# A spectral layer and a feed-forward network in one kernel: stage 1 of the first batch handed on within SBUF, and the start-up ranked anew

## The chip, the cores and the metric

The kernel runs on one core of a Trainium2 chip. The metric is the device time of one execution in microseconds: the median of three runs for the kernel before the change. In what follows PE is TensorE's matmul, PEld its weight load, DVE is VectorE, ACT is ScalarE, POOL is GpSimd, SP is SyncE, which here issues most DMAs. "L305" is line 305 of the kernel before the change.

## The reference

```
x: (8, 3008, 256) float32;  w_r, w_i: (256, 256);  b_r, b_i: (256)
X = rfft(x, axis=1)                               # along the sequence of 3008
Yr = Xr @ w_r - Xi @ w_i + b_r
Yi = Xr @ w_i + Xi @ w_r + b_i
Y  = soft threshold of both with lam = 0.01
y  = irfft(Y, n=3008, axis=1)                     # (8, 3008, 256), taken as 24064 tokens

h = y @ w_in                                      # w_in (256, 2048)
g = h * clip(h + 3, 0, 6) / 6
out = g @ w_out                                   # w_out (2048, 256), out (24064, 256) float32
```

The inputs `w_in` and `w_out` arrive as float64 and are decoded on the chip.

## The kernel before, in words

The sequence of 3008 is split into 64 x 47, so that the transform is one of length 47 and one of length 64. Half the spectrum is kept, NK = 24 of the 47 frequencies. The 64 rows are taken in seven sets (`SEGS`): six of 10 rows and one of 4. A set of 10 rows fills 120 partitions (5 rows x 24) with two groups of 256 columns.

For each batch b three stages make y:

- `stage1(b)` (L264): a set of x is loaded (`xin`, the part for "plus" and the part for "minus" side by side, 4 KB in a row), sum and difference are made, and a matmul with the tables of length 47 gives the cosine part (c = 0) and the sine part (c = 1). ACT copies each into a tile `a` (L303), and a DMA stores it to the DRAM scratch `scr1` (L305). For batch 0 this is plain fp32 without `split`, the stores are issued from ACT's queue, and `a` uses seven tags of other buffers in turn.
- `middle(b)` (L353): 12 steps over pairs of frequencies. Each loads `bt` from `scr1` (L367), where the 128 partitions are now (c, n1), and a table `f64` (L368); `s2` makes the transform of length 64 (L376); `s3` the mixing with w_r and w_i (L137, from `mixed`), bias and soft threshold (L414, L425, L426, L429), and turns the halves over into `zt` by four small DMAs within SBUF (L439), for the last two pairs of batch 0 by four DVE copies (L437); `s5` goes back over the length 64 (L453), is copied by ACT into `pt` (L455) and stored to `scr2` (L456).
- `segment(b, k)` (L477): loads `qt` from `scr2` (L486), goes back over the length 47 (L505) and writes y into `raw` (L513, L515, L527).

`prepare(c)` (L544) then makes the combinations of 512 tokens that the network wants, in tiles `yb`. The network runs over 376 units (47 blocks of 512 tokens x 8 slices f of the 2048 hidden columns): `phase_a` to `phase_d` multiply by `w_in` with seven products of half size in place of eight, `gate` makes the activation, and `down` multiplies by `w_out` (L631). Every fp32 operand is split into a high and a low part (`split`, L128: an ACT cast and a subtraction), and a product is three matmuls.

The weights are decoded in 16 bands of 512 KB: `in_band(f)` and `out_band(f)` for f = 0 to 7, in the order in0, in1, out0, in2, out1, in3, out2, in4, ... Each is a load `st` from SP (L178) and work on DVE, ACT and POOL (L190 to L222). `turn()` (L244) brings bands on; `EARLY` and `LATE` say in which borrowed buffers. Unit f needs in_band(f), and three units later out_band(f).

The order of the work in each engine's queue is not simply the order of the text. The framework schedules the instructions over a simulated timeline with the text's order as priority: an instruction whose operands and buffers are free earlier can be drawn ahead. `tc.high_priority()` ranks what it encloses first. After that the queues are fixed: each engine and each DMA-issuing queue works in order.

The start is written out by hand: stage 1 of batch 0, then the 36 steps of `middle(0)` with a `turn` every third, then the first two segments with `turn(LATE)` between, then `prepare(0)` (L647 to L663), then the loop over the units, in which `fill` places the later batches' stages at computed slots.

Of the kernel before, what the change touches and what calls it, by code (L numbers as in the profile page):

```python
# [1 line left out]

# [1 line left out]

# [5 lines left out]
F32 = mybir.dt.float32  # L10
F32R = mybir.dt.float32r
# [10 lines left out]
B, S, D, FF = 8, 3008, 256, 2048  # L22
N1, N2 = 64, 47
NK = N2 // 2 + 1
LAM = 0.01
P = 128

J = 5
SEGS = tuple((n1, min(2 * J, N1 - n1)) for n1 in range(0, N1, 2 * J))
R47 = J * NK  # L30
# [70 lines left out]
def spectral_ffn(ctx: ExitStack, tc: tile.TileContext, x, w_r, w_i, bias, w_in, w_out, f47, f64, g64, sgn, out):  # L101
    nc = tc.nc
    const = ctx.enter_context(tc.tile_pool(name="const", bufs=1))
    sb = ctx.enter_context(tc.tile_pool(name="sb", bufs=1))
    dram = ctx.enter_context(tc.tile_pool(name="dram", bufs=2, space=DRAM))
# [8 lines left out]
    def space(shape, dt, name, tag=None):  # L114
        tag = tag or name
        return sb.tile(shape, dt, name=name, tag=tag, bufs=depth.get(tag, 1))
# [11 lines left out]
    def split(hi, lo, src, on=None):  # L128

        nc.scalar.copy(out=hi, in_=src)  # L130
        (on or nc.vector).tensor_tensor(out=lo, in0=src, in1=hi.bitcast(F32), op=ALU.subtract)  # L131

    def product(ps, terms, start=True, stop=True, more=False):

        todo = [p for (ah, al), (bh, bl) in terms for p in ((al, bh), (ah, bl), (ah, bh))]
        for n, (a, b) in enumerate(todo):
            nc.tensor.matmul(  # L137
                out=ps,
                lhsT=a,
                rhs=b,  # L140
                start=start and n == 0,
                stop=stop and n == len(todo) - 1,
                skip_group_check=more,
            )
# [9 lines left out]
    def run(g):  # L154
        for _ in g:
            pass

    nf = NFT // 2
# [5 lines left out]

    win_s = [const.tile([P, nf, 7, P], F32R, name="w_in_" + t) for t in ("hi", "lo")]
    wout_s = [const.tile([P, NFT * D], F32R, name="w_out_" + t) for t in ("hi", "lo")]

    top = const.tile([P, 2], F32, name="top")  # L170
# [32 lines left out]
    def in_band(f, tags):  # L203
        def cut(t, words):
            v = t.rearrange("p (h c) -> p h c", h=2)
            return v[:, :, f * 256 * words : (f + 1) * 256 * words]

        w, s = yield from decode(w_in, cut, tags)
        s = s.rearrange("p a (b c) -> p (a b) c", b=2)
        a11, a12, a21, a22 = w[:, 0, :P], w[:, 1, :P], w[:, 0, P:], w[:, 1, P:]  # L210
        for to, a, b, op in (
            (0, a21, a22, ALU.add),
            (1, s[:, 0], a11, ALU.subtract),
            (2, a11, a21, ALU.subtract),
            (3, a12, s[:, 1], ALU.subtract),
        ):
            nc.gpsimd.tensor_tensor(out=s[:, to], in0=a, in1=b, op=op)
        yield
        hi, lo = (t[:, f] for t in win_s)
        split(hi[:, :2], lo[:, :2], w[:, :, :P])  # L220
        split(hi[:, 2], lo[:, 2], a22)
        split(hi[:, 3:], lo[:, 3:], s)  # L222
# [10 lines left out]
    EARLY = (("raw", "yb", "yb", "yb"),)  # L233
# [10 lines left out]
    def turn(how=None):  # L244

        for job in list(busy):
            if next(job[0], busy) is busy:
                busy.remove(job)
                ready.add(job[1])
        if how and made[0] < 2 * nf:  # L250
            make, f = next(bands)
            g = make(f, how[made[0] % len(how)])
            next(g)
            busy.append((g, (make, f)))
            made[0] += 1
# [6 lines left out]
    scr1, scr2 = {}, {}  # L262

    def stage1(b):  # L264
        scr1[b] = dram.tile([2, N1, NK, D], F32, name="scr1")
        sets = SEGS[-1:] + SEGS[:-1]
        xins = {}

        def load(i):
            n1, n = sets[i]  # L270
            rows, w = (R47, 2 * D) if n == 2 * J else (n * NK, D)
            tag = ("xin", "gs", None, "gs", None, "raw", "raw")[i] if b == 0 else "xin"
            if tag == "gs":
                xins[i], xins[i + 1] = twin([P, 2, 2 * D], F32, "xin", tag)
            elif tag:
                xins[i] = space([P, 2, 2 * D], F32, "xin", tag)
            at = n1 // J * 2 * D
            src = x[b, :rows, at : at + 2 * w].rearrange("p (s c) -> p s c", s=2)
            nc.sync.dma_start(out=xins[i][:rows, :, :w], in_=src)
            return rows, w  # L280

        shapes = [load(i) for i in range(len(sets))] if b == 0 else [load(0)]
        for i, (n1, n) in enumerate(sets):
            rows, w = shapes[i]
            xin = xins.pop(i)
            plus, minus = xin[:rows, 0, :w], xin[:rows, 1, :w]
            e = space([P, 2 * D], F32, "e", "r" if b == 0 else "e")[:rows, :w]
            (nc.vector if b == 0 else nc.gpsimd).tensor_tensor(out=e, in0=plus, in1=minus, op=ALU.add)  # L288
            (nc.vector if b == 0 else nc.gpsimd).tensor_tensor(out=plus, in0=plus, in1=minus, op=ALU.subtract)
            for c, src in enumerate((e, plus)):  # L290
                q = 2 * i + c
                if b == 0:
                    ps = room(c == 1)
                    turns = f47_s[2][:rows, c * R47 : c * R47 + rows]
                    nc.tensor.matmul(out=ps[:rows, :w], lhsT=turns, rhs=src, start=True, stop=True)
                else:
                    xs = [t[:rows, :w] for t in twin([P, 2 * D], F32R, "xs")]
                    split(*xs, src, nc.vector if b == 1 else nc.gpsimd)
                    yield
                    ps = room()  # L300
                    product(ps[:rows, :w], [([t[:rows, c * R47 : c * R47 + rows] for t in f47_s[:2]], xs)])
                a = space([P, 2 * D], F32, "a", ("a", "h", "z", "h", "xs", "h", "X")[q % 7] if b == 0 else "a")[:rows, :w]
                nc.scalar.copy(out=a, in_=ps[:rows, :w])  # L303
                dst = scr1[b][c, n1 : n1 + n].rearrange("(g j) k d -> (j k) g d", g=w // D)
                (nc.sync if b else nc.scalar).dma_start(out=dst, in_=a.rearrange("p (g d) -> p g d", d=D))  # L305
                if c and b and i + 1 < len(sets):
                    shapes.append(load(i + 1))
                yield
# [26 lines left out]
    for i, _ in enumerate(stage1(0)):  # L335
        if i == 7:
            r, k = [loaded(w, P, 2 * D, n, "yb") for w, n in ((w_r, "w_r"), (w_i, "w_i"))]
# [14 lines left out]

    def middle(b):  # L353
        scr2[b] = dram.tile([2, N1, NK, D], F32, name="scr2")
        src = scr1[b].rearrange("c n k d -> (c n) k d")
        dst = scr2[b].rearrange("c n k d -> (c n) k d")
        NG = NK // 2
        LAG = (1, 2, 3) if b else (2, 5, 5)
        bt, xs, zs = {}, {}, {}
# [3 lines left out]
            return tags[0 if b else g % 3]  # L363

        def load(g):
            bt[g] = space([P, 2, D], F32, "bt"), space([P, 2, P], F32, "f64")
            nc.sync.dma_start(out=bt[g][0], in_=src[:, 2 * g : 2 * g + 2, :])  # L367
            nc.sync.dma_start(out=bt[g][1], in_=f64.rearrange("p (k c) -> p k c", c=P)[:, 2 * g : 2 * g + 2])  # L368

        def s2(g):  # L370
# [86 lines left out]

        load(0)
        load(1)
        for g in range(NG + LAG[2]):  # L460
            if g >= LAG[2]:
# [79 lines left out]
    WEIGHT = {1: 0, 2: 1, 3: 6, 4: 2, 5: 3, 6: 4, 7: 5}  # L541
    yb = {}

    def prepare(c):  # L544
        y = raw.pop(c)
        b11, b12, b21, b22 = y[:, 0, :H], y[:, 0, H:], y[:, 1, :H], y[:, 1, H:]
        s = space([P, 4, H], F32, "T")
        for to, p, q in ((0, b12, b11), (1, b22, s[:, 0]), (2, b22, b12), (3, b21, s[:, 1])):
            nc.gpsimd.tensor_tensor(out=s[:, to], in0=p, in1=q, op=ALU.subtract)
        yield  # L550
        for n, src in ((2, b21), (1, b11), (6, s[:, 1]), (7, s[:, 2]), (5, s[:, 0]), (4, s[:, 3]), (3, b22)):
            t = space([P, 2, H], F32R, "yb")
            split(t[:, 0], t[:, 1], src, nc.vector if c == 0 and n in (1, 2) else nc.gpsimd)
            yb[c, n] = (t[:, 0], t[:, 1])
            yield
# [3 lines left out]

    def block(i, n, ps, start):  # L560
        c, f = units[i]
        product(ps, [(tuple(t[:, f, WEIGHT[n]] for t in win_s), yb[c, n])], start=start, more=True)

    def kept(i, n, ps):
        t = keep[i, n] = space([P, H], F32, n)
# [79 lines left out]


    mid = middle(0)  # L647
    for i in range(3 * (NK // 2)):
        next(mid)
        if i % 3 == 0:  # L650
            turn(EARLY if i == 3 or i % 9 == 0 else None)
    run(mid)
    first = [segment(0, k, tag) for k, tag in ((0, "qt"), (1, "h"))]
    for g in first:
        next(g)
    for n in range(3):
        turn(LATE)
        turn()
    for g in first:
        turn(LATE)  # L660
        run(g)
        turn()
    run(prepare(0))  # L663


    slots = {}
# [21 lines left out]
    for c in range(1, NC):  # L688
        g = prepare(c)
# [23 lines left out]
    n = len(units)  # L713
# [75 lines left out]
```

## Time and profile before

| | |
|---|---|
| median of three runs | 2643.61 us (2640.65 to 2645.09) |
| the profiled execution | 2643.59 us |
| its span | 2641.8 us |
| mean granted clock of TensorE | 0.988 |
| PE busy | 2562.4 us, 97% |
| PEld busy | 2291.9 us, 87% |
| DVE, ACT, POOL busy | 1975.7, 1820.1, 796.0 us |
| HBM read, written | 97.45 MB, 74.97 MB |

The span is the time from the first to the last instruction, 1.8 us less than the time of the same execution. The engines work side by side, so their busy times do not add up to the span. Lines of the timeline give the start, the time from the first start to the last end of a run of equal instructions, the engine, the line, the operation, written tile <- read tiles, shapes, the count, and in brackets the idle time of the engine before and what ended it. Lines of the waits give who waited for whom, the total, the number of times and the longest.

### The profile page before, as it was taken

The page shows a single profiled execution, that of the slowest core. Times are in us where ns is not written, and L with a number is a line of the kernel's source. Part 1 is how long each engine was busy: PE and PEld are TensorE (multiplying, and loading weights), DVE is VectorE, ACT ScalarE, POOL GpSimd, SP SyncE. Part 2 cuts the span into 40 slices and gives each one's busy share as a digit, 9 for nine tenths or more (in the row PEclk, how much of TensorE's full clock was granted, in tenths as well). Part 3 has the DMA queues.
Part 4 walks back from the last instruction along what each step waited for, and adds up shares of the span by engine and source line. Part 5 has one row for each costly group of instructions (what it writes and reads, how often), then busy time and mean ns, then how long its engine had stood idle before and what let it go on. Part 6 is the DMA issues. An engine that isn't in the chain of part 4 may idle for free.

```text
span 2641.8 us, 44527 instructions
## 1 busy us (share of the span) xinstructions
PE 2562.4 (97%) x16406; PEld 2291.9 (87%) x16406; DVE 1975.7 (75%) x3186; ACT 1820.1 (69%) x3592; POOL 796.0 (30%) x749
## 2 busy tenths in 40 slices
PE   5789999999999999999999999999999999999999
PEld 3577998988898998988898998999889889898887
DVE  7786886877677777777777777777777777666766
ACT  5476677767667777766776777677777666676766
POOL 2263334443233332233323333233321121121210
PEclk8889999999999999999999999999999999999999
DMA  7623333332223321323213322233221111100000
GB/s 216 191 79 93 103 104 94 113 107 75 59 60 96 88 69 48 85 78 90 73 49 86 88 76 63 76 84 84 63 79 58 50 53 53 43 26 30 12 17 17
DMA packets 150178, 199.98 MB, mean 76 GB/s; under 512 B 16847, under 2 KB 104135, under 8 KB 149959
## 3 DMA queue, kind: packets, MB, share of 16 engines
q1 hardware_dynamic: 146675, 193.98, 25.4%
q10 hardware_dynamic: 3284, 3.15, 0.4%
q8 instruction: 129, 2.11, 0.3%
q14 instruction: 90, 0.74, 0.1%
HBM read 97.45 MB, written 74.97 MB: 65 GB/s over the span
## 4 chain that ended last, share of the span: by engine, by line
PE 84%; DVE 4%; ACT 4%; DMA 2%; POOL 2%; issue 2%; SPq 0%; ACTq 0%; POOLq 0%; DVEq 0%
PE po L631 36%; PE pb L137 17%; PE ps_a L137 11%; PE pc L137 9%; PE pd L137 4%; PE ps_a L505 3%; PE ps_a L376 3%; ACT gs L130 1%; DMA xin<-in_x 1%; DVE r L610 1%; ACT r L608 1%; DVE gs L131 1%; POOL e L288 1%; DVE h L572 1%; POOL yb L131 0%
## 5 line engine op out<-in xcount | busy, mean ns | idle before, releaser
L631 PE MATMUL po<-gs,w_out_hi 128*128 128x512 f32 x3008 | 1006.5, 396 | 0.0
L610 DVE SCALAR_TENSOR_TENSOR r<-r,h 128x1024 f32<-128x1024 f32 x376 | 486.9, 1295 | 267.7 <-ACT r L608 265.9
L631 PEld LDWEIGHTS po<-gs,w_out_hi 128*128 128x128 f32 x3008 | 541.3, 188 | 85.5
L631 PE MATMUL po<-gs,w_out_lo 128*128 128x512 f32 x1504 | 601.9, 400 | 5.9 <-ACT gs L130 3.3
L608 ACT ACTIVATE r<-h,three 128x1024 f32<-128x1024 f32 x376 | 434.3, 1155 | 214.6 <-DVE h L572 211.6
L137 PE MATMUL pb<-yb,w_in_hi 128*128 128x256 f32 x3008 | 571.6, 279 | 2.5 <-POOL yb L131 2.5
L131 DVE TENSOR_TENSOR gs<-r,gs 128x1024 fp32r<-128x1024 f32 x376 | 484.4, 1288 | 80.7 <-ACT gs L130 78.8
L137 PEld LDWEIGHTS pb<-yb,w_in_hi 128*128 128x128 f32 x3008 | 461.0, 189 | 22.5 <-POOL yb L131 2.7
L130 ACT CAST gs<-r 128x1024 fp32r<-128x1024 f32 x376 | 395.8, 1053 | 92.5 <-DVE r L610 89.5
L572 DVE TENSOR_TENSOR h<-pc,u 128x256 f32<-128x256 f32 x752 | 315.1, 419 | 175.3 <-PE pc L137 160.1
L131 POOL TENSOR_TENSOR yb<-T,yb 128x256 fp32r<-128x256 f32 x188 | 181.0, 969 | 859.4 <-ACT yb L130 841.6
L137 PE MATMUL pb<-yb,w_in_lo 128*128 128x256 f32 x1504 | 431.3, 288 | 4.6 <-ACT p L567 1.6
L567 ACT COPY u<-pb 128x256 f32<-128x256 f32 x752 | 277.8, 373 | 121.5 <-PE pb L137 103.8
L631 PEld LDWEIGHTS po<-gs,w_out_lo 128*128 128x128 f32 x1504 | 284.0, 189 | 63.3 <-ACT gs L130 14.5
L137 PEld LDWEIGHTS pb<-yb,w_in_lo 128*128 128x128 f32 x1504 | 284.3, 189 | 29.7 <-ACT h L601 4.1
L137 PE MATMUL pc<-yb,w_in_hi 128*128 128x256 f32 x1504 | 297.6, 279 | 0.8 <-POOL yb L131 0.8
L137 PEld LDWEIGHTS pc<-yb,w_in_hi 128*128 128x128 f32 x1504 | 230.7, 189 | 13.3 <-POOL yb L131 1.1
L137 PE MATMUL pc<-yb,w_in_lo 128*128 128x256 f32 x752 | 219.0, 291 | 5.5 <-DVE h L572 4.9
L567 ACT COPY p<-pb 128x256 f32<-128x256 f32 x376 | 139.9, 372 | 80.9 <-PE pb L137 78.6
L601 ACT COPY h<-pb 128x256 f32<-128x256 f32 x376 | 140.5, 374 | 57.4 <-PE pb L137 55.4
L572 DVE TENSOR_TENSOR h<-pd,p 128x256 f32<-128x256 f32 x376 | 156.7, 417 | 14.9 <-ACT p L567 10.2
L137 PEld LDWEIGHTS pc<-yb,w_in_lo 128*128 128x128 f32 x752 | 142.1, 189 | 21.7 <-DVE h L572 7.9
(125 smaller groups left out, 3928.9 us busy)
## 6 DMA issues: line engine op xcount, KB each, us to landing
bt<-scr SPq DMA_DIRECT2D x96, 256.0 KB, 2.9
scr<-pt SPq DMA_DIRECT2D x96, 256.0 KB, 2.4
zt<-tc SPq DMA_DIRECT2D x376, 64.0 KB, 2.0
out<-ot SPq DMA_DIRECT2D x94, 256.0 KB, 2.3
xin<-in_x SPq DMA_DIRECT2D x48, 480.0 KB, 4.8
qt<-scr SPq DMA_DIRECT2D x96, 240.0 KB, 3.5
scr<-a SPq DMA_DIRECT2D x84, 240.0 KB, 2.5
f<-in_f SPq DMA_DIRECT2D x96, 128.0 KB, 2.8
```

Of the source, the lines that this page charges most:

```text
L130: nc.scalar.copy(out=hi, in_=src)
L131: (on or nc.vector).tensor_tensor(out=lo, in0=src, in1=hi.bitcast(F32), op=ALU.subtract)
L137: nc.tensor.matmul(out=ps, lhsT=a, rhs=b, start=start and n == 0, stop=stop and n == len(todo) - 1, skip_group_check=more,)
L288: (nc.vector if b == 0 else nc.gpsimd).tensor_tensor(out=e, in0=plus, in1=minus, op=ALU.add)
L376: nc.tensor.matmul(out=psv[:, dh, :, u, :], lhsT=data[:, u, dh * P : (dh + 1) * P], rhs=f[:, u, :], start=True, stop=True,)
L505: nc.tensor.matmul(out=ps[:, cs * w + g * rows : cs * w + (g + 1) * rows], lhsT=qt[:rows, cs, g, dh * P : (dh + 1) * P], rhs=f47_s[2][:row ...
L567: nc.scalar.copy(out=t, in_=ps)
L572: nc.vector.tensor_tensor(out=to, in0=ps, in1=keep.pop((i, n)), op=ALU.add)
L601: nc.scalar.copy(out=hs[i][:, 1, :H], in_=pb)
L608: nc.scalar.activation(out=r, in_=h, func=AF.Relu, bias=three, scale=1.0)
L610: nc.vector.scalar_tensor_tensor(out=r, in0=r, scalar=6.0, in1=h, op0=ALU.min, op1=ALU.mult)
L631: nc.tensor.matmul(out=pos[dh], lhsT=w[:, ft * D + dh * P : ft * D + (dh + 1) * P], rhs=g[:, low, u], start=f == 0 and u == 0 and which == ...
```

## The change

- Batch 0's stage 1 no longer goes through DRAM. Each result `a` is written by DMAs into an SBUF area `spread`, with (c, n1) on the partitions and 24 x 256 numbers in each: one DMA for each group of 5 rows, so that 120 partitions of 1 KB go into 5 partitions of 24 KB. Group 0 is issued from ACT, group 1 from SP. The copies out of PSUM and these DMAs are ranked first. `middle(0)` reads its pairs from `spread`, with no `bt` load.
- `spread` lies in the place of the `w_in` slices that are decoded last: high and low parts now share one tile, the low ones in reversed order, and `spread` covers positions 4 to 10 of 16: the high parts of f = 4 to 7 and the low parts of f = 7, 6 and 5. These can be written only when the last stage 2 product has read its pair.
- x is laid out with all "plus" parts of a row ahead of all "minus" parts, so a set is loaded as two packets of 2 KB for each partition instead of one of 4 KB.
- `EARLY` is used at seven of the 36 steps instead of five.
- The rest of `middle(0)` after the 36 steps, the first two segments and `prepare(0)` are ranked first.

```diff
-    win_s = [const.tile([P, nf, 7, P], F32R, name="w_in_" + t) for t in ("hi", "lo")]
+    win_t = const.tile([P, 2 * nf, 7, P], F32R, name="w_in")
+    win_s = [[win_t[:, f] for f in range(nf)], [win_t[:, 2 * nf - 1 - f] for f in range(nf)]]
+    spread = win_t[:, nf // 2 : nf // 2 + 7].rearrange("p f s c -> p (f s c)").bitcast(F32)
+    spread = spread[:, : NK * D].rearrange("p (k d) -> p k d", d=D)
...
-            at = n1 // J * 2 * D
-            src = x[b, :rows, at : at + 2 * w].rearrange("p (s c) -> p s c", s=2)
+            at = n1 // J * D
+            src = x[b, :rows].rearrange("p (s c) -> p s c", s=2)[:, :, at : at + w]
...
-                nc.scalar.copy(out=a, in_=ps[:rows, :w])
-                dst = scr1[b][c, n1 : n1 + n].rearrange("(g j) k d -> (j k) g d", g=w // D)
-                (nc.sync if b else nc.scalar).dma_start(out=dst, in_=a.rearrange("p (g d) -> p g d", d=D))
+                with tc.high_priority() if b == 0 else nullcontext():
+                    nc.scalar.copy(out=a, in_=ps[:rows, :w])
+                if b:
+                    dst = scr1[b][c, n1 : n1 + n].rearrange("(g j) k d -> (j k) g d", g=w // D)
+                    nc.sync.dma_start(out=dst, in_=a.rearrange("p (g d) -> p g d", d=D))
+                else:
+                    for g in range(w // D):
+                        at = c * N1 + n1 + g * J
+                        queue = nc.sync if g else nc.scalar
+                        with tc.high_priority():
+                            queue.dma_start(out=spread[at : at + rows // NK], in_=a[:, g * D : (g + 1) * D])
...
-            bt[g] = space([P, 2, D], F32, "bt"), space([P, 2, P], F32, "f64")
-            nc.sync.dma_start(out=bt[g][0], in_=src[:, 2 * g : 2 * g + 2, :])
+            bt[g] = space([P, 2, D], F32, "bt") if b else spread[:, 2 * g : 2 * g + 2], space([P, 2, P], F32, "f64")
+            if b:
+                nc.sync.dma_start(out=bt[g][0], in_=src[:, 2 * g : 2 * g + 2, :])
...
-            turn(EARLY if i == 3 or i % 9 == 0 else None)
-    run(mid)
+            turn(EARLY if i == 0 or i % 6 == 3 else None)
+    def ahead(g):
+        with tc.high_priority():
+            run(g)
+
+    ahead(mid)
     first = [segment(0, k, tag) for k, tag in ((0, "qt"), (1, "h"))]
     for g in first:
-        next(g)
+        with tc.high_priority():
+            next(g)
...
-        run(g)
+        ahead(g)
         turn()
-    run(prepare(0))
+    ahead(prepare(0))
...
-    pairs = half[:, :, :12].reshape(B, R47, 6, 2, 2, D).transpose(0, 1, 2, 4, 3, 5)
-    xp = np.zeros((B, R47, 32 * D), np.float32)
-    xp[:, :, : 24 * D] = pairs.reshape(B, R47, 24 * D)
-    xp[:, :, 24 * D : 26 * D] = half[:, :, 12].reshape(B, R47, 2 * D)
+    xp = np.zeros((B, R47, 2, 16, D), np.float32)
+    xp[:, :, :, :13] = half.transpose(0, 1, 3, 2, 4)
+    xp = xp.reshape(B, R47, 32 * D)
```

More of the change, by code (lines that the diff above doesn't have):

```diff
@@ L1 @@
-from contextlib import ExitStack
+from contextlib import ExitStack, nullcontext
 import numpy as np
@@ L218, in in_band @@
         yield
-        hi, lo = (t[:, f] for t in win_s)
+        hi, lo = (t[f] for t in win_s)
         split(hi[:, :2], lo[:, :2], w[:, :, :P])
@@ L264, in stage1 @@
     def stage1(b):
-        scr1[b] = dram.tile([2, N1, NK, D], F32, name="scr1")
+        if b:
+            scr1[b] = dram.tile([2, N1, NK, D], F32, name="scr1")
         sets = SEGS[-1:] + SEGS[:-1]
@@ L354, in middle @@
         scr2[b] = dram.tile([2, N1, NK, D], F32, name="scr2")
-        src = scr1[b].rearrange("c n k d -> (c n) k d")
+        src = scr1[b].rearrange("c n k d -> (c n) k d") if b else None
         dst = scr2[b].rearrange("c n k d -> (c n) k d")
@@ L365, in load @@
         def load(g):
-            bt[g] = space([P, 2, D], F32, "bt"), space([P, 2, P], F32, "f64")
-            nc.sync.dma_start(out=bt[g][0], in_=src[:, 2 * g : 2 * g + 2, :])
+            bt[g] = space([P, 2, D], F32, "bt") if b else spread[:, 2 * g : 2 * g + 2], space([P, 2, P], F32, "f64")
+            if b:
+                nc.sync.dma_start(out=bt[g][0], in_=src[:, 2 * g : 2 * g + 2, :])
             nc.sync.dma_start(out=bt[g][1], in_=f64.rearrange("p (k c) -> p k c", c=P)[:, 2 * g : 2 * g + 2])
@@ L561, in block @@
         c, f = units[i]
-        product(ps, [(tuple(t[:, f, WEIGHT[n]] for t in win_s), yb[c, n])], start=start, more=True)
+        product(ps, [(tuple(t[f][:, WEIGHT[n]] for t in win_s), yb[c, n])], start=start, more=True)
     def kept(i, n, ps):
```

## The prediction

> **What bounds the kernel now.** I read the page first, then the busy time by stretches of the span.
>
> ```profile
> span 2641.8 us, 44527 instructions
> PE 2562.4 (97%) x16406; PEld 2291.9 (87%) x16406; DVE 1975.7 (75%) x3186; ACT 1820.1 (69%) x3592; POOL 796.0 (30%) x749
> 0.00:20.00 20.00, 9.81 (x15) 4.03 (x16) 8.98 (x17) 4.20 (x8) 0.20 (x4) 1.00 0.89 229
> 20.00:40.00 20.00, 8.39 (x14) 2.52 (x12) 11.57 (x20) 14.18 (x28) 3.88 (x5) 0.76 0.91 297
> 40.00:60.00 20.00, 13.77 (x85) 13.51 (x86) 20.00 (x29) 12.00 (x24) 13.32 (x16) 0.64 0.45 147
> 80.00:100.00 20.00, 18.57 (x137) 16.48 (x136) 9.80 (x16) 6.50 (x12) 0.00 (x0) 1.00 0.67 198
> 100.00:120.00 20.00, 11.37 (x56) 7.06 (x54) 17.07 (x33) 11.21 (x21) 4.81 (x6) 0.81 0.63 196
> 140.00:160.00 20.00, 14.34 (x68) 12.37 (x69) 17.60 (x29) 14.28 (x34) 20.00 (x20) 0.75 0.30 86
> 260.00:2642.00 2382.00, 2364.66 (x15316) 2129.72 (x15314) 1785.30 (x2886) 1665.50 (x3289) 700.75 (x649) 1.00 0.24 68
> ```
>
> The rows give start and end of a stretch, its length, then busy PE, PEld, DVE, ACT and POOL, the granted clock, the DMA share and GB/s. TensorE is idle 2641.8 - 2562.4 = 79.4 us in all. From 260 us on only 2382.0 - 2364.7 = 17.3 us of that are left, so 62 us lie in the first 260 us. The steady loop is full of matmuls that the change does not touch: what it wins or loses is the moment at which the first blocks of the network start, and every microsecond there moves the end by about as much. In the first 40 us the DMA engines are the busiest (0.89 and 0.91), from 40 to 60 us DVE is (20.00 of 20), from 80 to 100 us PE is (18.57), and then DVE (17.07 of 20 from 100 us on) and POOL (20.00 of 20 from 140 us on). The waits of PE within the first 260 us name the holes:
>
> ```profile
> PE pb L376 <- ACT m L197: 12.3, 1, 12.3
> PE ps_a L505 <- DMA qt<-scr: 7.2, 1, 7.2
> PE pb L453 <- DVE zt L437: 5.6, 1, 5.6
> PE pb L376 <- DMA f<-in_f: 1.4, 1, 1.4
> PE pb L453 <- DMA zt<-tc: 1.4, 2, 1.2
> ```
>
> The first is the wait between stage 1 and stage 2 of batch 0. It is put down to ACT, but the rows of the timeline show the way through DRAM:
>
> ```profile
> 31.07 0.59 ACT L303 COPY a<-pb 120x512 f32<-120x512 f32 x1
> 31.20 1.41 ACTq L305 DMA_DIRECT2D scr<-a  x2
> 37.23 0.81 SPq L367 DMA_DIRECT2D bt<-scr  x2
> 41.45 3.75 PE L376 MATMUL pb<-f,bt 128*128 128x128 f32 x16 [12.30 <-ACT m L197]
> 49.98 0.58 PE L137 MATMUL ps_a<-w_r_hi,X 128*128 128x256 f32 x1 [4.78 <-DVE X L131]
> ```
>
> The last copy ends at 31.66, the last stores are issued by 32.6, the loads behind them go out at 37.23, and PE starts at 41.45.
>
> **The change, part by part.**
>
> (a) Stage 1 of batch 0 stays in SBUF. Each 240 KB store becomes two DMAs of 120 KB, one on ACT's queue and one on SP's, and a 96 KB store one: 26 DMAs for 14. SP gets 12 more issues, ranked first, each behind the wait for its copy, and the band loads and f loads stand behind them there. The copies can run only seven ahead of the DMAs, since `a` has seven tags. What a DMA costs comes from the first 140 us of the DMA view:
>
> ```profile
> q10 hardware_dynamic: 3284, 3.15, 6.8%
> scr<-a ACTq DMA_DIRECT2D x12, 240.0 KB, 5.0
> scr<-a ACTq DMA_DIRECT2D x2, 96.0 KB, 7.7
> bt<-scr SPq DMA_DIRECT2D x12, 256.0 KB, 3.2
> zt<-tc SPq DMA_DIRECT2D x40, 64.0 KB, 2.2
> ```
>
> Best end: the nearest copy within SBUF, zt<-tc, lands 2.2 us after its issue. 32.6 + 2.2 = 34.8, so stage 2 would start about 35.0 instead of 41.45: -6.4 us. Worst end: each queue has 13 of the DMAs, and if one waits for the other at the 5.0 us of the present stores that is 65 us; counted from about 7 us, when x is being loaded (the window 4 to 8 us, below), the end is near 72: +30 us. The truth hangs on how many DMA engines work on one DMA. Queue q10 carries these 14 stores alone: 12 x 240 + 2 x 96 = 3072 packets of 1 KB, and 3284 - 3072 = 212 small ones are left, which is 12 x 15 + 2 x 16, one end mark per engine: 15 engines for 120 rows, 16 for 96. A copy into 64 rows shows 16 marks beside its 64 packets:
>
> ```profile
> DMA packets 80, 0.07 MB, mean 94 GB/s; under 512 B 16, under 2 KB 80, under 8 KB 80
> ```
>
> So the number follows the rows, and the new DMAs write 5 rows (4 in the first set). I come back to that among the rivals. DVE was full from 40 to 60 us and held the first mixing product to 49.98, so up to 5 us of a later stage 2 would be covered, as the bands go on meanwhile. Between -6.4 and +30 I take 0: the round trip saved (6.4 us) and the crowding on few engines (+9, below) are of one size, and the cover of 5 us stands between them.
>
> The Trainium skill speaks against this part: in DMA: Bandwidth & Descriptors, section "Why a DMA increments its semaphore by 16 and not by 1", a DMA gets the largest number of engines up to 16 that divides the slowest dimension of both its sides. The 15, 16 and 16 marks agree with it. By it the new DMAs have five or four, and the time is that of the slower rival, 2658; without it 2635.6 or less.
>
> (b) The x loads go in 2 KB packets. Their present packets are of 4 KB, and these windows are 4 to 8 us (x alone) and 36.0 to 37.4 us (mostly weight loads of 2 KB):
>
> ```profile
> DMA packets 269, 0.97 MB, mean 243 GB/s; under 512 B 28, under 2 KB 28, under 8 KB 269
> DMA packets 290, 0.54 MB, mean 387 GB/s; under 512 B 22, under 2 KB 59, under 8 KB 290
> ```
>
> Batch 0's six sets of 120 rows of 4 KB and one of 96 rows of 2 KB, 3072 KB, take 13 us at 243 GB/s and 8.1 us at 387. Ends: 0 (the rate belongs to x and its rows, not to the packet) and -5 us. I take 0, because stage 1's pace after 16 us is set by its own DMAs; what there is of it is in (a)'s lower half. For the later batches x loads are far ahead of need: nothing.
>
> (c) The 12 bt loads fall away: 12 x 256 KB and 12 issues of SP (0.81 us for two, above). They delay the f loads behind them; the only stall of PE there is 1.4 us (pb L376 <- DMA f<-in_f). Ends 0 and -3 (twice that, for the zt copies on the same queue, 1.4 us in the same view of waits): I take -1.
>
> (d) The end of batch 0's middle, the first segments and the first blocks of y rank first. This is the tail as it runs now, in the lines of the timeline that belong to it:
>
> ```profile
> 106.85 0.28 PE L137 MATMUL ps_a<-w_r_hi,X 128*128 128x256 f32 x1
> 107.62 0.58 DVE L437 COPY zt<-tc 64x256 f32<-64x256 f32 x2
> 108.23 0.69 DVE L414 TENSOR_TENSOR tc<-ps_a,bias 128x512 f32<-128x512 f32 x1
> 110.18 0.43 DVE L425 TENSOR_SCALAR tc<-tc 128x512 f32<-128x512 f32 x1
> 112.06 0.68 DVE L426 TENSOR_TENSOR tc<-tc 128x512 f32<-128x512 f32 x1
> 112.78 0.51 ACT L429 ACTIVATE tc<-tc,sgn 128x256 f32<-128x256 f32 x1 [0.77 <-DVE tc L426]
> 114.34 2.49 DVE L437 COPY zt<-tc 64x256 f32<-64x256 f32 x4
> 116.98 2.04 PE L453 MATMUL pb<-zt,g_all 128*128 128x512 f32 x2 [5.59 <-DVE zt L437]
> 121.98 1.81 SPq L486 DMA_DIRECT2D qt<-scr  x4
> 126.22 3.77 PE L505 MATMUL ps_a<-f_all,qt 120*128 120x120 f32 x16 [7.19 <-DMA qt<-scr]
> 129.17 0.36 ACT L513 COPY odd<-ps_a 128x240 f32<-128x240 f32 x1 [1.62 <-PE ps_a L505]
> 131.26 0.40 DVE L515 TENSOR_TENSOR raw<-ps_a,odd 128x240 f32<-128x240 f32 x1
> 132.06 3.74 PE L505 MATMUL ps_a<-f_all,qt 120*128 120x120 f32 x16 [2.08 <-issue]
> ```
>
> The chain's DVE work waits in line: 108.23 - 107.13 = 1.1; 110.18 - 108.92 = 1.3; 112.06 - 110.61 = 1.4; 114.34 - 113.29 = 1.1; and the four copies take 2.49 us instead of the 1.16 us of two such pairs at 107.62 (0.58), 1.3. Together 6.2 us in which DVE does bands. In the segments, 131.26 - 129.53 = 1.7 us, and about 0.4 for the next: 2.1. So -8.3 if rank is kept on the chip; the way through DRAM (116.98 to 126.22) stays. Ends -8.3 and 0; I take -8, as nothing but lower-ranked bands stood in between.
>
> (e) What is ranked behind pays. Those 8.3 us of band work come later, into 140 to 160 us, where POOL is full and DVE at 17.60 of 20, and PE is busy for 14.34 of 20. Ends 0 and +8.3; I take +1: the bands of units 4 to 7 are due only some 27 us and more after the first block (376 units in the 2500 us from 140 us on, 6.7 us each).
>
> (f) Seven early bands for five. Bands 4 to 7 of w_in lie under the staged data and cannot be written before the last stage 2 product. The two more early ones (DVE and POOL were at 9.80 and 0.00 of 20 from 80 to 100 us) take the place of those. Ends -8.3 and +8.3, the one amount of band work measured on this path; I take 0. The lo halves in reversed order and the single tile cost nothing: the matmuls keep their shapes, and no instruction is added.
>
> Sum: 0 + 0 - 1 - 8 + 1 + 0 = -8 us. The profiled execution took 2643.59 us (span 2641.8 and 1.8 around it), the median is 2643.61, so one base serves both: 2635.6 us.
>
> **The rivals.** 0.2%, 5.3 us, is about what a measurement of this kernel can tell from no change.
>
> Slower: the new DMAs are held to five engines. The 3072 packets cost 0.068 x 140 us x 16 engines = 152 us of engine time, 50 ns each. Now 152 / 15 = 10 us per engine; on five, each has 24 x 24 + 2 x 24 = 624 packets, 31 us. That is 21 us more on each of the five in a stretch where their share is 0.9. From 41.45, less 4.2 us for the loads that go, plus 21: 58; less 4 us for the idle tenth: 54. With 5 us of DVE's cover a is +8 to +9; if packets into neighbouring rows also get in each other's way, it goes toward the +30 worked out in (a). It decides from a = +13.3 on, where it outweighs the 8 us and 5.3 more. 2643.6 + 22 - 8 = 2658. For it: the marks. Against: what shares that stretch with them, the band loads above all, can give way without PE waiting for it.
>
> The Trainium skill's SBUF — State Buffer, section "Door 1: The DMA port swizzle", puts four neighbouring partitions on one port and shows 27.6 GB/s for partitions 0 to 3; as an estimate from that page, a DMA of 96 to 120 KB into so few rows takes about 3.5 us, so 13 per queue take 46 us, and stage 2 would start near 55: a = +14, the time 2650. No run here shows a write into so few rows.
>
> Quicker: all engines serve, or the rest keeps up: a = -6.4, and 2643.6 - 14.4 = 2629; with (b)'s 5 us 2624.
>
> Hidden: the tail is quicker, but the displaced bands stop the first units (e at +8.3), or DVE's bands hold stage 2 as before: 2643.
>
> **Chances.** Forecast 0.36 (its own range 2628 to 2641), quicker 0.22, hidden 0.13, slower 0.29. Of the forecast's case about a quarter ends within 5.3 us: faster 0.36 x 0.75 + 0.22 = 0.49; same 0.36 x 0.25 + 0.13 = 0.22; slower 0.29. The range reaches to 2618 (quicker, with (b) and the two early bands gained) and to 2660, which leaves out the outer part of the slow case, under 0.1, and little below.
>
> **What would show it.** (a): PE's first stage 2 product (now 41.45) within 5 us of that, no bt<-scr issue before it, and the number of small packets in ACT's queue, which gives the engines: near 5 per DMA or near 15. If the slow case holds, the wait of pb L376 is over 20 us and DMA share in that stretch falls to a third. (d): the gap from the last mixing product to the first segment product falls from 19.1 us to 13. (e): PE busy from 140 to 160 us stays above 14. Wrong it is if stage 2 starts after 55 us, or if the first block's gain is gone by 260 us.

## The result, and the profile after

The changed kernel is slower. Its median is 2673.66 us (2671.23 to 2676.39, four runs) against 2644.35 us for the kernel before (2640.65 to 2645.44, four runs): 1.0114 times by the ratio on record, 95% interval 1.0096 to 1.0131, which is about 30 us. The prediction said 2635.6 us and a range up to 2660.

The profiled execution of the changed kernel took 2676.39 us. In its page and its stretches of time (columns as before: start and end, length, busy PE, PEld, DVE, ACT, POOL, clock, DMA share, GB/s):

```profile
span 2674.2 us, 44529 instructions
PE 2568.8 (96%) x16406; PEld 2294.4 (86%) x16406; DVE 1976.6 (74%) x3186; ACT 1817.4 (68%) x3592; POOL 781.6 (29%) x749
0.00:20.00 20.00, 10.03 (x18) 3.97 (x18) 8.18 (x16) 4.27 (x8) 0.20 (x4) 1.00 0.85 191
20.00:40.00 20.00, 7.60 (x10) 2.55 (x10) 2.79 (x5) 4.91 (x9) 0.00 (x0) 0.71 0.38 97
40.00:60.00 20.00, 0.00 (x0) 0.00 (x0) 2.79 (x5) 3.59 (x7) 0.00 (x0) 0.50 0.54 131
140.00:160.00 20.00, 7.57 (x25) 5.49 (x25) 12.69 (x26) 10.39 (x21) 7.79 (x11) 0.52 0.59 177
260.00:2674.00 2414.00, 2391.36 (x15447) 2150.45 (x15445) 1808.99 (x2909) 1680.46 (x3324) 696.08 (x658) 1.00 0.24 68
```

PE is idle for 2674.2 - 2568.8 = 105.4 us instead of 79.4: 26.0 of the 32.4 us by which the span grew. The other 6.4 us are PE's own busy time, for the same 16406 matmuls; why they take longer was not looked into. From 260 us on it is idle for 22.6 us instead of 17.3, so 20.7 of the 26.0 us are lost at the start. From 20 to 60 us no compute engine is busy for more than two fifths of a stretch: before, DVE had 11.57 and 20.00 us of work in these two stretches and the DMA share was 0.91 in the first, now DVE has 2.79 twice and the share is 0.38 and 0.54. The waits of PE within the first 300 us, below them that of ACT's copies up to 62 us, and the timeline of the place:

```profile
PE pb L389 <- DMA st<-in_w_in: 23.7, 1, 23.7
PE pb L299 <- ACT a L308: 12.2, 2, 6.8
PE ps_a L137 <- DVE X L131: 10.7, 3, 7.5
...
ACT a L308 <- DMA w_in<-a: 21.5, 6, 7.7
```

```profile
33.51 0.58 ACT L308 COPY a<-ps_a 120x512 f32<-120x512 f32 x1 [4.85 <-DMA w_in<-a]
44.15 4.68 ACTq L317 DMA_DIRECT2D w_in<-a  x2
53.27 3.26 SPq L181 DMA_DIRECT2D st<-in_w_in  x3
61.27 3.75 PE L389 MATMUL pb<-f,w_in 128*128 128x128 f32 x16 [23.68 <-DMA st<-in_w_in]
64.72 0.58 PE L137 MATMUL ps_a<-w_r_hi,X 128*128 128x256 f32 x1
```

The first line of the waits puts the 23.7 us down to a load of a band, the last semaphore to come. The timeline shows what it stands for: the copies out of PSUM wait for the DMAs of `a` (`w_in<-a`, since `spread` lies in `w_in`; 21.5 us in six waits), and the last of these DMAs is issued by 49.1 us. By the trace's packet records the last packets of 1 KB (those of `a`, and of the table `f64` behind them) end at 60.93 us on SP's queue, 0.3 us before stage 2 starts: it is these that PE waits for. Only behind the last issue does SP reach the loads of the bands: the first is issued at 53.27 us, the first one before was issued at 19.43 us:

```profile
19.43 13.75 SPq L178 DMA_DIRECT2D st<-in_w_in  x4
```

(That line is of the timeline of before.) Stage 2 starts at 61.27 instead of 41.45, the first block of the network at 162.99 instead of 135.51, and the span ends 32.4 us later.

The table has the main moments of the start: PE's first stage 2 product, its first mixing product, the end of the last mixing product, the first block's first product, and the span, all in us of the profiled executions, each of which lies within 2.8 us of its kernel's median. The ratio is the one on record, with its interval; it is not exactly the quotient of the two medians. Each experiment was timed with the kernel before beside it on one chip, where before took 2640.55 us (e1 to e4), 2641.98 us (e5 and the three `_only`) or 2642.10 us (r2, three_early, four_early).

| kernel | stage 2 | mixing | mixing ends | block | span | time to before |
|---|---|---|---|---|---|---|
| before | 41.45 | 49.98 | 107.13 | 135.51 | 2641.8 | |
| after | 61.27 | 64.72 | 135.43 | 162.99 | 2674.2 | 1.0114 [1.0096, 1.0131] |
| e1_dram | 38.63 | 46.94 | 113.55 | 141.68 | 2647.8 | 1.0036 [1.0023, 1.0049] |
| e2_scatter | 61.14 | 64.59 | 130.84 | 159.68 | 2665.3 | 1.0104 [1.0087, 1.0121] |
| e3_rows120 | 34.34 | 38.42 | 111.04 | 137.76 | 2646.8 | 1.0022 [1.0013, 1.0032] |
| e4_ports | 50.59 | 54.04 | 124.78 | 151.73 | 2662.3 | 1.0083 [1.0068, 1.0098] |
| e5_pool_ports | 79.02 | 86.40 | 145.94 | 172.44 | 2681.5 | 1.0166 [1.0150, 1.0181] |
| r2_rows120 | 29.55 | 37.85 | 107.68 | 136.22 | 2642.8 | 1.0007 [0.9998, 1.0016] |
| x_only | 38.95 | 46.92 | 108.47 | 135.40 | 2643.4 | 1.0015 [1.0006, 1.0023] |
| rank_only | 40.93 | 49.59 | 106.07 | 134.47 | 2639.4 | 1.0002 [0.9993, 1.0011] |
| seven_only | 40.99 | 48.73 | 113.20 | 143.18 | 2641.7 | 1.0018 [1.0009, 1.0027] |
| four_early | 40.27 | 49.47 | 105.20 | 133.45 | 2644.2 | 1.0019 [1.0010, 1.0028] |
| three_early | 40.77 | 48.71 | 103.21 | 131.69 | 2649.7 | 1.0031 [1.0019, 1.0044] |

### The profile page after: what moved, and what is told of

It reads as the page before. It is cut to its first block, busy times and chain, and to the rows that moved or that the text cites. A ratio compares the mean times of both kernels' runs of the same rounds, so it can differ in the third digit from the quotient of the medians.

```text
span 2674.2 us, 44529 instructions
## 1 busy us (share of the span) xinstructions
PE 2568.8 (96%) x16406; PEld 2294.4 (86%) x16406; DVE 1976.6 (74%) x3186; ACT 1817.4 (68%) x3592; POOL 781.6 (29%) x749
## 4 chain that ended last, share of the span: by engine, by line
PE 81%; DVE 6%; ACT 4%; DMA 4%; issue 2%; POOL 2%; SPq 0%; ACTq 0%; DVEq 0%; POOLq 0%
PE po L644 35%; PE pb L137 17%; PE ps_a L137 10%; PE pc L137 9%; PE pd L137 4%; PE ps_a L518 3%; PE ps_a L389 3%; DMA xin<-in_x 2%; ACT gs L130 2%; DVE r L623 2%; ACT r L621 1%; DMA w_in<-a 1%; DVE gs L131 1%; DVE h L585 1%; DVE tc L439 1%
## 5 line engine op out<-in xcount | busy, mean ns | idle before, releaser
L137 PE MATMUL pb<-yb,w_in 128*128 128x256 f32 x4512 | 704.3, 282 | 4.8 <-POOL yb L131 1.7
L137 PEld LDWEIGHTS pb<-yb,w_in 128*128 128x128 f32 x4512 | 631.9, 189 | 49.6 <-ACT p L580 3.5
L137 PE MATMUL pc<-yb,w_in 128*128 128x256 f32 x2256 | 394.7, 283 | 3.2 <-DVE h L585 2.7
L137 PEld LDWEIGHTS pc<-yb,w_in 128*128 128x128 f32 x2256 | 336.7, 189 | 31.5 <-DVE h L585 6.2
L137 PE MATMUL pd<-yb,w_in 128*128 128x256 f32 x1128 | 198.6, 283 | 2.1 <-DVE h L585 1.8
L137 PEld LDWEIGHTS pd<-yb,w_in 128*128 128x128 f32 x1128 | 165.5, 189 | 12.3 <-DVE h L585 4.4
L292 POOL TENSOR_TENSOR e<-xin 120x512 f32<-120x512 f32 (+1 forms) x49 | 68.3, 1394 | 279.5 <-DMA xin<-in_x 279.5
L131 POOL TENSOR_TENSOR xs<-xin,xs 120x512 fp32r<-120x512 f32 (+1 forms) x42 | 55.3, 1317 | 308.7 <-ACT xs L130 259.1
```

The source lines that it names most:

```text
L137: nc.tensor.matmul(out=ps, lhsT=a, rhs=b, start=start and n == 0, stop=stop and n == len(todo) - 1, skip_group_check=more,)
```

## The experiments

**Which part costs the time.** e1_dram is the changed kernel with batch 0's stage 1 through DRAM again; the ranks, the x layout and the seven early bands stay.

```diff
...
-                if b:
-                    dst = scr1[b][c, n1 : n1 + n].rearrange(...)
-                    nc.sync.dma_start(out=dst, in_=...)
-                else:
-                    for g in range(w // D):
-                        ...  queue.dma_start(out=spread[at : at + rows // NK], in_=a[:, g * D : (g + 1) * D])
+                dst = scr1[b][c, n1 : n1 + n].rearrange(...)
+                with tc.high_priority() if b == 0 else nullcontext():
+                    (nc.sync if b else nc.scalar).dma_start(out=dst, in_=...)
...
```

> All of the change but the way within SBUF: batch 0's stage 1 goes through DRAM again (stores on ACT's queue, ranked first, bt loads in the middle). If the five engines of the new DMAs are the whole cause, the first stage 2 product is back at 40 to 43 us (61.3 in the changed kernel, 41.5 before) and the time at 2636 to 2646, so that the rest of the change is worth 0 to -8 us. If the ranking or the seven bands cost time of their own, stage 2 starts at 40 to 43 us too, but the time stays at 2650 or more.

It took 2651.34 us, 1.0036 times before. In its profile PE is idle for 79.5 us, as before; the 6.0 us by which the span is longer are busy time (2568.3 us instead of 2562.4). e2_scatter is the other half: the kernel before with the way within SBUF alone (`spread`, the 26 DMAs, the ranked copies), the old x layout, five early bands, no rank for the tail.

> The kernel before with the way within SBUF alone (no new x layout, five early bands, no new ranks behind stage 1). Five engines: 14 DMAs on ACT's queue with 12 x 5 + 2 x 4 = 68 end marks, first stage 2 product at 57 to 63 us, time 2664 to 2678. If it needs the ranks or the bands to be slow: stage 2 before 50 us and 2640 to 2655.

It took 2668.52 us, 1.0104 times: 27.5 us of the 30. Stage 2 starts at 61.14, as in the changed kernel. So the way within SBUF carries the loss. By itself the rest costs 9.5 us by e1_dram; the two do not simply add up (37 us against 30), so the rest costs less beside the scatter than alone; that the wait which the scatter makes covers it is likely but not shown.

**Why: the number of engines, the rows, or the DMAs as such.** e3_rows120 issues the same 26 DMAs, of the same bytes, at the same places in the queues, but each writes all its 120 (96) rows. It leaves out the turn from rows to (c, n1), so its output is wrong and only its time says something; and a pair of stage 2 then needs two DMAs and no longer all of them.

```diff
...
-                        at = c * N1 + n1 + g * J
+                        k = 12 * c + n1 // J + g
+                        to = spread[8 * c : 8 * c + rows, k] if n == 2 * J else aside[:rows, c]
...
-                            queue.dma_start(out=spread[at : at + rows // NK], in_=a[:, g * D : (g + 1) * D])
+                            queue.dma_start(out=to, in_=a[:, g * D : (g + 1) * D])
```

> The changed kernel with the same 26 DMAs on the same queues, but each writes its 120 (96) rows into as many rows of the area instead of five: the turn from rows to (c, n1) is left out, so stage 2 reads numbers in the wrong places. Engines: 12 x 15 + 2 x 16 = 212 marks on ACT's queue, first stage 2 product at 35 to 40 us, time 2630 to 2645. If instead the order in the queues of ACT and SP (12 more issues, band and f loads behind them) is the cause, stage 2 stays after 50 us and the time above 2660.

Stage 2 starts at 34.34 us, and the time is 2646.74 us. By the trace the last of the 26 DMAs lands at 34.0 us, so that a pair needs only two of them won next to nothing here. Neither the number of DMAs nor their queues, then, but the rows into which they write. The queue of ACT alone, in the DMA view of the first 140 us (packets, MB, share of 16 engines), first of the changed kernel and then of e3_rows120:

```profile
q10 hardware_dynamic: 1700, 1.67, 4.8%
```

```profile
q10 hardware_dynamic: 1844, 1.67, 4.5%
```

The queue carries 12 x 120 + 2 x 96 = 1632 packets of 1 KB. The rest are end marks: 1700 - 1632 = 68 = 12 x 5 + 2 x 4 in the changed kernel, 1844 - 1632 = 212 = 12 x 15 + 2 x 16 here. Five engines against fifteen.

e4_ports keeps five rows and so five engines, but takes rows 24 apart instead of neighbours; the table `f64` of batch 0 is laid out in the same order of rows.

```diff
...
-                        at = c * N1 + n1 + g * J
+                        m = 12 * c + n1 // J + g
+                        to = spread[m : m + 97 : 24] if n == 2 * J else spread[120 + 4 * c : 124 + 4 * c]
```

> The changed kernel with each group of five rows laid 24 rows apart instead of side by side (the table of stage 2 of batch 0 in the same order, so the same result). Still five engines: 68 marks. If the number of engines decides, stage 2 starts at 52 to 58 us, since only the packets get shorter (57 to 65 ns now, 46 at best), and the time is 2660 to 2670. If neighbouring rows in one another's way decide, stage 2 starts before 45 us and the time is below 2648.

Stage 2 starts at 50.59 us, and the time is 2664.11 us, 1.0083 times. In the DMA view from 30 to 40 us, where nearly only these DMAs run, the changed kernel:

```profile
DMA  3223333333333333333333333334333333322222
DMA packets 988, 0.95 MB, mean 95 GB/s; under 512 B 40, under 2 KB 988, under 8 KB 988
q1 hardware_dynamic: 533, 0.51, 17.7%
q10 hardware_dynamic: 455, 0.45, 15.3%
```

and e4_ports, whose queue of ACT takes 3.8% of the first 140 us instead of 4.8%:

```profile
DMA  3333333333333333333333333333333333333333
DMA packets 1195, 1.18 MB, mean 118 GB/s; under 512 B 47, under 2 KB 1195, under 8 KB 1195
q1 hardware_dynamic: 629, 0.62, 17.9%
q10 hardware_dynamic: 566, 0.56, 16.0%
```

Both have a third of the 16 engines at work, whatever is in flight on two queues: five of 16 are 0.31. Had each queue its own five, the share could be twice that; all these DMAs thus share the same five. The same five engines move 118 GB/s into rows 24 apart and 95 into neighbours. So the way from 61.27 to 34.34 has two parts: 10.7 us for neighbouring rows (61.27 - 50.59) and 16.3 us for five engines instead of fifteen (50.59 - 34.34; which rows are written changes with the engines there).

e5_pool_ports issues the 26 DMAs of e4_ports from POOL (`queue = nc.gpsimd`), to see whether another queue gets other engines.

> The run with the five rows 24 apart, with its 26 DMAs issued by POOL instead of ACT and SP. If the DMAs that POOL issues also sit on the same five engines, stage 2 starts at 50 us or later and the time is 2660 or more. If POOL's DMAs spread over other engines from one to the next, stage 2 starts at 36 to 42 us and the time is 2645 to 2653, that is near the run through DRAM.

It is the slowest of all, 2685.3 us, and stage 2 starts at 79.02 us. From its timeline:

```profile
6.42 1.50 POOL L325 DMA_DIRECT2D w_in<-a  x2 [5.97 <-ACT a L315]
59.23 0.63 POOL L325 DMA_DIRECT2D w_in<-a  x1 [1.84 <-issue]
60.24 0.64 POOL L325 DMA_DIRECT2D w_in<-a  x1 [0.38 <-issue]
65.74 0.63 POOL L325 DMA_DIRECT2D w_in<-a  x1 [4.86 <-issue]
72.53 0.64 POOL L325 DMA_DIRECT2D w_in<-a  x1 [0.61 <-issue]
79.02 1.19 PE L397 MATMUL pb<-f,w_in 128*128 128x128 f32 x4 [47.82 <-DMA w_in<-a]
```

Each issue takes POOL about 0.64 us, 26 of them 17 us, but they are spread from 6.4 to 73.2 us, with gaps in most of which POOL waits for nothing that the profile shows. The DMA view from 20 to 48 us, in 40 slices of 0.7 us:

```profile
DMA  9999999998988975307963530035320134300243
q0 software_dynamic: 1314, 1.44, 21.6%
```

In its second half, where little but POOL's queue (q0) is at work, stretches of three to five tenths alternate with slices in which nearly no engine is busy. So the pauses between the issues hold the data back there, and not the engines alone. What fills the pauses, and whether POOL's DMAs got other engines than the five, stays open: the first branch of the expectation is met in its numbers, not in its reason.

**Would a quick way within SBUF have paid?** r2_rows120 is e2_scatter (five early bands, old x layout, no ranks for the tail) with the 120-row DMAs of e3_rows120: the way within SBUF as if it had all engines.

> The kernel before with the way within SBUF alone, each DMA into 120 (96) rows instead of five, as in the earlier run with that edit (the turn is left out, so stage 2 reads numbers in the wrong places), but with five early bands and x as before. It says what the way within SBUF would be worth without the five engines: stage 2 at 34 to 37 us. If those 5 to 7 us arrive at the end: 2635 to 2638. If DVE's bands take them: first block at 133 us or later and the time within 0.2% of before.

It took 2644.12 us, 1.0007 times before, with an interval that holds 1. Stage 2 starts 11.9 us earlier (29.55, ahead of the 34 to 37 that were expected), the mixing ends 0.6 us later. Two things in its timeline limit what it can say:

```profile
29.55 2.11 PE L393 MATMUL pb<-f,w_in 128*128 128x128 f32 x16
30.94 1.74 ACTq L321 DMA_DIRECT2D w_in<-a  x2
32.98 0.67 SPq L184 DMA_DIRECT2D st<-in_w_in  x1
```

The first pair of stage 2 needs only two DMAs here, as in e3_rows120, so stage 2 starts before the last ones are issued; by the trace those land at 34.5 us, and a kernel that needs all of them could win 6.9 us there (41.45 - 34.52), not 11.9. So this run is kinder to the way within SBUF than the real case. On the other hand the first band load goes out at 32.98 us instead of 19.43, because the new DMAs stand ahead of it on SP's queue. The stretch up to stage 2 and the stretch from there to the end of the mixing, of before and of r2_rows120:

```profile
0.00:41.45 41.45, 18.19 (x29) 6.57 (x29) 22.00 (x39) 19.32 (x36) 4.38 (x10) 0.87 0.89 259
41.45:107.13 65.68, 57.70 (x402) 52.34 (x402) 48.74 (x79) 30.46 (x57) 16.08 (x18) 0.90 0.59 178
```

```profile
0.00:29.55 29.55, 17.98 (x29) 7.10 (x29) 10.88 (x20) 8.70 (x16) 5.51 (x6) 0.88 0.84 218
29.55:107.68 78.13, 59.79 (x402) 53.66 (x402) 62.52 (x105) 45.98 (x86) 26.58 (x30) 0.91 0.57 171
```

DVE has 22.00 + 48.74 = 70.7 us to do up to the end of the mixing before, and 10.88 + 62.52 = 73.4 us here: nearly the same work. Before, 22 of it ran ahead of stage 2, 11 more than here; the wait was of use. Here nearly all of its band part comes after the start of stage 2, and PE's middle grows by 12.5 us with it. That DVE's bands are what makes the middle longer is read from these sums, and the runs with other numbers of early bands agree (44.00 us of DVE in a middle of 62.44 in three_early, 57.28 in 72.21 in seven_only). What a quick way would be worth with the band loads issued as early as before, no run shows. The same rows of the changed kernel:

```profile
0.00:61.27 61.27, 17.62 (x28) 6.54 (x29) 13.76 (x25) 12.77 (x24) 0.20 (x4) 0.73 0.60 143
61.27:135.43 74.16, 59.91 (x402) 53.75 (x402) 65.03 (x107) 43.22 (x82) 30.00 (x31) 0.90 0.53 157
```

Here PE waits longer and DVE does less up to stage 2 (13.76 us in 61 instead of 22.00 in 41), because no band has arrived; 65.03 us are left for a middle that took 48.74.

**The three other parts, each alone on the kernel before.** seven_only:

```diff
-            turn(EARLY if i == 3 or i % 9 == 0 else None)
+            turn(EARLY if i == 0 or i % 6 == 3 else None)
```

> The kernel before with seven early bands instead of five, nothing else. The run through DRAM with the rest of the change took 74.9 us from the first stage 2 product to the last mixing product (65.7 before) and started the first block 6.2 us later. If the additional early bands do that by their work on DVE in the middle, this run shows 72 us or more in that stretch, more band loads before 65 us than the eight of before, and 2644 to 2652. If the ranking is the cause, the stretch stays at 64 to 68 us and the time within 0.2%.

2645.94 us, 1.0018 times. The first block starts 7.7 us later; DVE has 79.2 us up to the end of the mixing (21.92 + 57.28) instead of 70.7:

```profile
0.00:40.99 40.99, 18.56 (x29) 7.01 (x29) 21.92 (x39) 19.39 (x36) 4.41 (x10) 0.79 0.90 261
40.99:113.20 72.21, 62.09 (x403) 55.94 (x404) 57.28 (x95) 38.90 (x72) 22.73 (x25) 0.88 0.58 177
```

To see whether fewer bands would then be better, three_early and four_early use `i % 12 == 0` and `i % 9 == 0` in the same place.

> The kernel before with three early bands (every twelfth step). If each early band lengthens the middle by its work on DVE, the stretch from the first stage 2 product to the last mixing product falls below 65.7 us and the first block starts before 135 us; the time is 2636 to 2642, lower only if the later bands then do not stop the first units. If five is where both hold each other in balance, the first block is earlier but the time is within 0.2% of before, or above 2647.

> The kernel before with four early bands (every ninth step). Between three and five on the same line: first block 131 to 136 us, time 2638 to 2644; if the number acts through a wholly different order of the queues rather than through DVE's work, the first block does not lie between those of three and five.

2649.93 and 2646.34 us, 1.0031 and 1.0019 times. The first block starts the earlier the fewer bands precede it: 131.69 with three, 133.45 with four, 135.51 with five, 143.18 with seven. The time does not follow: five is the least, and the kernel whose first block comes earliest has the longest time of the four, though its interval overlaps with those of seven and four. The bands left out come later: three_early's last three loads go out at 133.24, 140.24 and 154.65 us, after its first block has begun; before, the last two went out at 136.64 and 139.65. That this is what costs the time is argued: PE is idle for 80.7 us in three_early and for 79.4 before, and the rest of the difference is busy time.

rank_only has the ranks for the tail alone, x_only the x layout alone (both as in the diff of the change).

> The kernel before with the ranking of the last pairs, the first segments and the first blocks of y alone. The prediction's step d: the last mixing product to the first segment product falls from 19.1 us to 13 and the time to 2633 to 2637. If the rank is not kept on the chip or only shifts the bands: 17 to 20 us and within 0.2% of before. If the ranking harms: the first block later than 138 us and the time above 2646.

> The kernel before with x in packets of 2 KB alone. By the prediction's step b the rate belongs to x's rows and not to the packet: 4 to 8 us still near 243 GB/s, stage 2 at 41 to 42 us, time within 0.2%. If the packet decides: near 380 GB/s, stage 2 at 36 to 39 us, time 2636 to 2640. If the doubled number of packets delays the stores: stage 2 after 43 us.

rank_only is the same as before, 1.0002 times, and the reason is plain: on PE, DVE, ACT and POOL it has the same instructions in the same order, one for one, and on SP the same DMAs. The rank moved nothing; why the framework kept the order was not looked into. Its timeline in the tail still has bands (L191, L195, L199) between the steps of the chain (L425, L426, L437):

```profile
108.57 0.43 DVE L425 TENSOR_SCALAR tc<-tc 128x512 f32<-128x512 f32 x1
108.91 0.42 DVE L191 TENSOR_SCALAR m<-st 128x512 int32<-128x512 int32 x1
109.25 0.69 DVE L195 SCALAR_TENSOR_TENSOR e<-st,e 128x512 int32<-128x512 int32 x1
109.85 0.68 DVE L199 SCALAR_TENSOR_TENSOR m<-m 128x512 f32<-128x512 int32 x1
110.45 0.68 DVE L426 TENSOR_TENSOR tc<-tc 128x512 f32<-128x512 f32 x1
111.05 1.75 DVE L199 SCALAR_TENSOR_TENSOR m<-m 128x512 f32<-128x512 int32 x1
112.73 2.50 DVE L437 COPY zt<-tc 64x256 f32<-64x256 f32 x4
```

x_only took 2645.45 us, 1.0015 times. From 4 to 8 us, where x is loaded, its rate is no better than before (243 GB/s there):

```profile
DMA packets 483, 0.94 MB, mean 235 GB/s; under 512 B 21, under 2 KB 27, under 8 KB 483
```

Stage 2 starts 2.5 us earlier and the first block as before, yet it ends some 4 us later (0.0015 x 2642). The order of the instructions is another one on all engines; from 260 us on PE is idle for 24 us (2643.4 - 260 - 2359.3) against 17, but over the whole execution it is idle no longer than before (78.7 against 79.4), so idle time alone is not the cause. What costs the 4 us was not found.

These three make 1.0018, 1.0002 and 1.0015 times, together 0.35%; e1_dram, which has all three and the ranked copies and stores of stage 1 besides, 0.36%. None of the runs beat the kernel before.

## Why the prediction was wrong, step by step

**(a), the way within SBUF, is the step that failed: taken at 0, it measured +27.5 us by itself (e2_scatter).** The mechanism stood in the text as the rival "slower", with its marks and its signs: the wait of pb over 20 us (23.7), the DMA share at a third (0.33), near five marks per DMA (68 for 14). What spoke for it, the 15, 16 and 16 marks per 120, 96 and 64 rows, was already a count in the profile; that the new DMAs write five rows was certain from the diff. It deserved the main place, not 0.29. The 0 itself was the middle of two cases that exclude each other, -6.4 with all engines and +9 with five; and the cover of 5 us, which was to stand between them, was already within the +9. The Trainium skill's DMA: Bandwidth & Descriptors, section "Why a DMA increments its semaphore by 16 and not by 1", had it right: five and four engines.

Within the rival two terms were too small. First, a packet was taken at 50 ns from the old stores. In the changed kernel ACT's queue takes 0.048 x 140 x 16 / 1632 = 66 ns, so 3072 packets need 3072 x 66 / 5 = 40 us of each of the five engines, not 31; with rows 24 apart it is 0.038 x 140 x 16 / 1632 = 52 ns and 32 us. The rival's stage 2 at 54 us holds for e4_ports (50.59), which has the packets at the price that was assumed, and the dearer packets are worth some 9 us (40.6 - 31.9) of the 10.7 by which the changed kernel comes later, at 61.27. That neighbouring rows get in each other's way was named, without a term. The Trainium skill's SBUF — State Buffer, section "Door 1: The DMA port swizzle", points the same way, as 118 against 95 GB/s shows; the estimate worked out from it, stage 2 near 55 us, was short by 6.

Second, the "cover of 5 us", because "the bands go on meanwhile". They did not. The prediction itself says that the band loads stand behind the new DMAs on SP's queue, and then did not draw the consequence: the first band load went out at 53.27 instead of 19.43 us, and DVE, full from 40 to 60 us before, had 2.79 us of work. The 8.5 us between stage 2 and the first mixing product did shrink to 3.5, the 5 us as forecast, but the bands that had filled the wait then ran in the middle: from the start of stage 2 to the end of the mixing 74.16 us instead of 65.68 (69.70 in e2_scatter, with five bands).

Nor did a run show the best end of (a), -6.4 us. In r2_rows120 stage 2 comes 11.9 us earlier and the time stays. The rival "hidden" comes nearest, though the bands lengthened the middle and did not hold the start of stage 2. With the band loads behind the new DMAs on SP's queue "quicker" (2629) was not to be had; with them ahead it was not tried. The sentence that every microsecond by which the first blocks start earlier moves the end by about as much is wrong as a rule. It holds for e2_scatter (first block +24.2, span +23.5), where all work moves. It fails in three_early, which puts off band work that is due later: its first block comes 3.8 us earlier and its time is about 8 us longer.

**(b)** was taken at 0 for the rate, and the rate did not change (243 to 235 GB/s, 228 in the changed kernel over the same 4 us). The 4 us that x_only lost are outside the range of that term (0 to -5), and their cause is open.

**(c)**, the loads of `bt` that go, was not tried alone; nothing of the -1 us can be seen beside the rest.

**(d), the rank of the tail, failed: -8 us were forecast, 0 was measured.** The reading of the waits in DVE's queue was sound, but the step from there to a gain assumed that rank decides the order in the queue ("nothing but lower-ranked bands stood in between"). In rank_only it moved no instruction. The gap from the last mixing product to the first segment's product, 19.1 us before, was to fall to 13; it is 18.3 in rank_only and 17.7 in the changed kernel. **(e)**, the price of displaced bands, had therefore no cause. PE's 7.57 us from 140 to 160 us are not that: the same part of the work now lies 27.5 us later, and from 167.5 to 187.5 us PE is busy for 16.73 us.

**(f)** was taken at 0 between -8.3 and +8.3 and measured +4.7 us (0.0018 x 2642). The 8.5 us more of DVE work before the end of the mixing are the band work of the upper end; the first block paid 7.7 of it, and the steady loop gave some 3 back.

The sum by measured parts is +27.5 + 4.7 + 4.0 + 0.5 = 37 us, and the whole is +30. That was above the range, whose upper end of 2660 left out the outer part of the slow case, which is what came.

## What to carry to other kernels

Before a transfer is turned into one that gathers rows, count the rows of the narrower side: the end marks of transfers that are already in the trace told here how many engines a row count gets, and the same few engines carried all the new transfers of both queues. A wait on the critical path may be worth only what no other engine uses it for: add up the work of the next engine (here DVE, 71 to 73 us to the end of the mixing) over the wait and the stage behind it, and check that its inputs still arrive when loads stand behind new transfers. A rank counts only once the order of the instructions is seen to change.

## What the runs showed of the hardware that was not expected

Five engines move 95 GB/s into five neighbouring rows and 118 into rows 24 apart, with the same share of busy engines. DMAs issued from POOL cost it 0.64 us each, with gaps of 0.3 to 10.8 us before the next, so that 26 took 67 us. And PE's granted clock is 0.50 in a stretch without matmuls (40 to 60 us of the changed kernel), still 0.76 in the next 20 us:

```profile
60.00:80.00 20.00, 11.73 (x80) 11.57 (x80) 16.75 (x26) 12.75 (x25) 9.14 (x11) 0.76 0.51 169
```
